# A gated mix of a long convolution and a dilated local attention: projection in halves, convolution with three buffers, and another order of loads and requests

## The chip, the cores and the metric

The kernel runs on one core of one Trainium2 chip. The core has five engines, each with its own in-order list of instructions: TensorE (PE in the profile; its weight loads are PEld), VectorE (DVE), ScalarE (ACT), GpSimd (POOL) and SyncE (SP). SyncE, ScalarE and GpSimd also issue DMA transfers, which 16 DMA engines carry out. The metric is the device time of one execution in microseconds, median of several; less is better.

## What is computed

The inputs have 2048 positions and 640 channels, in bf16. With x = q, the output is g * a + (1 - g) * b, in short:

```python
g = sigmoid((x * gate_w).sum(-1, keepdims=True))
# a: a short convolution of 4 taps on k, times v, then a long convolution over all positions
k_shift = sum(k_pad[:, t:t+S, :] * shift_k[:, 3 - t] for t in range(4))
kv = k_shift * v
y  = irfft(rfft(kv, 2*S) * rfft(ssm_k, 2*S))[:S] + kv * ssm_D
a  = q * y
# b: attention of 32 heads of 20 channels, each position looks at 8 positions, 2 apart
q_, k_, v_ = split(x @ wqkv)
attn = softmax(q_ . k_[pos - 2*w] * 20**-0.5, w = 0..7)
b = (attn . v_[pos - 2*w]) @ wo
```

## The kernel before

The attention half. Even and odd positions are taken apart, so that a head looks at 8 neighbours in a row. `xpose` turns x (tile `xn`) into `xT` by TensorE. `qkproj` makes q and k (five tiles `ft` of 128 columns, first with `Wqk`'s first 128 columns and then the rest), evicted into `stg`; `vproj` makes v in two halves of 320 columns (tile `psv`, evicted into `VW`). `fragger` copies each head's 20 rows from `stg` into a set of four heads (`kb`, `qb`), by DMA issued from GpSimd (line 583). The sets already hold, in other rows, factors that make the mask: GpSimd's `masks` (lines 362 to 365) spreads them from the small tile `mm` over three sets, at the start of the kernel, ahead of the first head's copy on GpSimd's list. Then `score_gen` multiplies (tile `sc`, line 607), ScalarE takes the exponential into `ETall` (line 614), `pv_gen` multiplies by v (tile `O`, line 637), and VectorE divides (lines 647 and 650). There are 80 such groups of scores. `op_tr` and `outproj` (tiles `tr`, `op`, `bl`) are the projection by `wo`.

The convolution half. `conv` (line 453) makes the four taps on VectorE: it first rearranges the tap weights, which GpSimd's queue loads from `shift_k` (line 406), by the copy of line 455, and then works on pieces of CR rows of k (tile `KX`), from the last row to the first. In `taps` a multiplication (line 440) writes one of two buffers, and an addition (line 447) adds it to the other. k arrives in three parts (`KROWS`), the first of them, rows 42 to 63, at the start. `conv_v` multiplies by v. The long convolution is a transform by matrices in two steps on TensorE (`h_stream`, `u_stream`, tiles `H`, `SX`, `UC`, `s`), a product on VectorE (line 717) and an inverse (line 796, tile `i`; last step line 877, `final`).

What sets the order. Each part is a Python generator that asks for its next request: TensorE, or ScalarE or VectorE for an eviction, and so on. The string `ORDER` grants these requests one by one (a letter for each generator, "-" ahead of it for the second engine named, VectorE), and the instructions are written in that order; nothing is decided while the kernel runs. Costs in the requests and the numbers in `LAND` and `STARTS` are not used by the chip: they are what the string was worked out from. Every engine works through its list in order, and waits where an operand is not there. TensorE's results go through four pairs of PSUM banks, which the evictions free.

`heads` (line 367) issues what comes first: the first loads from the queues of ScalarE and SyncE, the small loads of GpSimd, and the masks.

Of the kernel before, what the change touches and what calls it, by code (L numbers as in the profile page):

```python
# [12 lines left out]
ACT = mybir.ActivationFunctionType  # L13
ALU = mybir.AluOpType
# [3 lines left out]
S = 2048  # L18
D = 640
# [3 lines left out]
NDT = 5  # L23
# [94 lines left out]
fcddccfcccccccxfdccfedddcccciccccdxxxeicxxxcccffcfccffdeffffxddxdddxx-xddffdffdiiddddxxeddeddfiddd-idi-idddeecccddilddddd-iicccycy  # L118
yf-icccc-yxycfcccccccccc-xfccccccyyyiydcccdeicc-yyyeycyiidddffdxddddxid-ideeddffdidddddcccc-iiffciyyeddecdfiddcd-idccdccccccfccffi
yyyyfici-ii-idddceddddeccccjdddffdidcdjdiedgddcccdigedddgdcccii-idycdccde-ydeddy-yccyycyddd-ydy-yyylyjdcecyccccccdjgdccdddjyceddd  # L120
-yydd-ydddz-zzzz-zzzeeddyd-yyddd-yz-zddzzz-zzzz-zzzedddzjdedd-zccddddzd-zdeedzddd-zz-zddzddde-zddddedz-zzzzjzeeqzzz-z000-00z00oopo
oooo-z00-0110-00001o-1o0000-0111-11101-010-0001o10-0110-0000oo11022211oooor-rpr2rr20-r0r1-r1112r-r2200o2011s0s22222222u001111s2s11
22o2111ss1ss111111o2ou4444444oo4ss33443333s333334444444444u33333333333u555suuuvuuuuuuuvvv5v5-5v5-55vvvvv555v55555-555ttst-tsssttvv
tt-ttttsss-sttt-ttsttts-tttssttttttsss-ssttst-ttts-st
"""


# [70 lines left out]
def kernel(  # L198
# [14 lines left out]
    nc = tc.nc  # L213
# [44 lines left out]
    pab = pab.rearrange("p (a n c) -> p a n c", a=2, c=QC)  # L258
# [28 lines left out]
    def ev(name):  # L287
        if name not in E:
            E[name] = Ev()
        return E[name]  # L290
# [5 lines left out]
    def at(name, t):  # L296
        ev(name).src, ev(name).lag = -1, t

    st = {}
# [67 lines left out]
    def heads():  # L367
# [6 lines left out]
        nc.scalar.dma_start(mm[:], ca["mm"].ap())  # L374
        for w in range(2):
            nc.scalar.dma_start(Wqk[:, :, w, 0:128], W3[:, :, w, 0:128])
            at(f"W0{w}", LAND["W0"])
        nc.scalar.dma_start(Wv[:, :, 0:320], W3[:, :, 2, 0:320])
        at("Wv0", LAND["Wv0"])
        at("ET", 4000.0)  # L380
        for a in range(8):
            nc.sync.dma_start(xn[:, a], raw(x2, 256 * a * D, [[2 * D, 128], [D, 2], [1, D]]))
            at(f"x{a}", LAND["x"][a])
        for w in range(2):
# [4 lines left out]
        n0, n1 = KROWS[0]  # L389
        for q in range(4):  # L390
            nc.sync.dma_start(kin[32 * q:32 * q + 32, 3 + n0:3 + n1, :], raw(k2, n0 * D + QC * q, [[64 * D, 32], [D, n1 - n0], [1, QC]]))
        for q in range(4):
            at(f"k0{q}", LAND["k"][0])
# [43 lines left out]
    def taps(eng, n, m, ta, tb, dst):  # L437
        def tap(d, j):
            w = wl[:, j, :].unsqueeze(1)
            eng.tensor_tensor(d, kin[:, n + 3 - j:n + 3 - j + m, :], w.to_broadcast([128, m, QC]), ALU.mult)  # L440

        tap(ta, 3)
        for j in (2, 1, 0):
            yield
            tap(tb, j)
            yield
            eng.tensor_tensor(ta if j else dst, ta, tb, ALU.add)  # L447

    def vmul(eng, n, m, c, ks):
        v_ = vin[:, c, n:n + m, :]  # L450
# [2 lines left out]
    def conv():  # L453
        yield Req("D", 570.0, [ev("k00")])
        nc.vector.tensor_copy(wl, wraw.rearrange("p c j -> p j c"))
        hi = 64
        while hi:
            m = min(CR, hi)
            n = hi - m
            c0 = 150.0 + 0.54 * m * QC  # L460
            need = [k for k, (n0, n1) in enumerate(KROWS) if n0 < hi and n1 > n - 3]
            g = yield Req("D", c0, [ev(f"k{k}{q}") for k in need for q in range(4)] + ([ev(f"kh{q}{a}") for q in range(4) for a in (1, 17)] if n < 3 else []))
            for _ in taps(nc.vector, n, m, pab[:, 0, 0:m], pab[:, 1, 0:m], kin[:, n + 3:n + 3 + m, :]):
                g = yield Req("D", c0)
            hi = n
        mark("convD", g)

# [352 lines left out]
    def outproj():  # L820
        yield Req("N", 0.0, [ev("oTall"), ev("wo"), ev("gate")])
        bl = p0.tile([128, 16, D], BF, name="bl", tag="VW")
        st["bl"] = bl
        wo, oT = st["wo"], st["oT"]
        for t in range(16):
            g = yield Req("P", 0.0, [ev(f"oT{ft}") for ft in range(NDT)], take=1, pe=(10, 149.0, 280.0, 133.0))
            op = psum(g, "op", (128, 1024))
            for ft in range(NDT):
                for n0, n1 in ((0, 512), (512, 640)):
                    nc.tensor.matmul(op[:, n0:n1], lhsT=oT[:, ft].rearrange("p h m a -> p a (h m)")[:, t, :], rhs=wo[:, ft, n0:n1],  # L830
                                     start=(ft == 0), stop=(ft == NDT - 1), skip_group_check=True)
            r = yield Req("AD", dict(A=680.0, D=740.0), [g.done], give=g.banks)
            if r.eng == "A":
                nc.scalar.activation(bl[:, t, :], op[:, 0:D], ACT.Copy, scale=omg[:, t:t + 1])
            else:
                nc.vector.tensor_scalar(bl[:, t, :], op[:, 0:D], omg[:, t:t + 1], None, ALU.mult)
            mark(f"bl{t}", r)
        mark("outproj", g)

# [95 lines left out]
```

## Time and profile before

| | us |
|---|---|
| median of 3 runs (225.1 to 226.12) | 226.06 |
| the profiled execution's own time | 226.44 |
| its span, from the first to the last instruction | 224.5 |
| TensorE busy | 204.4 (91%) |
| VectorE busy | 183.1 (82%) |
| ScalarE busy | 171.0 (76%) |
| GpSimd busy | 69.0 (31%) |

The granted TensorE clock is 0.999 over the span. The stages: to 31 us the transposes and first projections; 31 to 143 us scores, exponentials and values, with the convolution, the other projections and the transform of the filter in between; 143 to 197 us the transform of the signal, the products, the output projection and the inverse; then the final stage with the output's DMAs. In the profile a row of the timeline has the start, the length, the engine, the line, the operation, the tiles written and read, the number of instructions, and in brackets how long the engine had stood and what ended it. In the chain of waits a row is a stretch of the chain that ended last. TensorE's busy time includes the time that a matmul takes to run out, so 91% is not 91% of its peak.

### The profile page before, as it was taken

To read this page: it belongs to the slowest core of one execution; us is meant where nothing else is said; L and a number is where in the kernel's file an instruction comes from. 1 tells how busy PE (TensorE), PEld (TensorE's weight loads), DVE (VectorE), ACT (ScalarE), POOL (GpSimd) and SP (SyncE) were. 2 spreads that over 40 slices of the span, in tenths; PEclk is the share of its full clock that TensorE was granted. 3 is DMA by queue.
4 is the path that set the end of the run, shared out by engine and by line. 5 is a ranking of instruction groups with operands and counts; after the bars stand their busy time and mean duration, and the time that the engine had idled before them with its cause. 6 is when DMAs were issued, how large, how long until landed. Compare 5 with 4: busy or idle time off the path is not lost.

```text
span 224.5 us, 8412 instructions
## 1 busy us (share of the span) xinstructions
PE 204.4 (91%) x3644; PEld 160.9 (72%) x3653; DVE 183.1 (82%) x236; ACT 171.0 (76%) x208; POOL 69.0 (31%) x154
## 2 busy tenths in 40 slices
PE   6799979999999979999998889879999999979890
PEld 2687966689776756666676667778987989967660
DVE  4533564889988966999899988999999997769982
ACT  2475437776978589879899989899999989755640
POOL 1999961534007614072360000000120094000000
PEclk9999999999999999999999999999999999999999
DMA  6999459999999989849944085584969404004544
GB/s 211 359 339 199 83 133 194 175 163 163 194 184 217 190 148 145 118 110 164 177 109 141 14 217 127 117 216 116 243 145 194 109 12 104 20 3 103 139 125 109
DMA packets 69020, 33.83 MB, mean 151 GB/s; under 512 B 51096, under 2 KB 66600, under 8 KB 68984
## 3 DMA queue, kind: packets, MB, share of 16 engines
q1 hardware_dynamic: 63192, 26.79, 57.0%
q0 software_dynamic: 3536, 5.69, 11.6%
q10 hardware_dynamic: 2256, 0.83, 1.5%
q8 instruction: 28, 0.46, 1.0%
q14 instruction: 8, 0.07, 0.1%
HBM read 20.01 MB, written 2.62 MB: 101 GB/s over the span
## 4 chain that ended last, share of the span: by engine, by line
PE 40%; DVE 21%; POOL 11%; issue 11%; DMA 8%; ACT 6%; ACTq 0%; DVEq 0%; POOLq 0%
PE pj L535 9%; PE i L796 8%; PE s L685 5%; ACT ETall L614 4%; PE O L637 4%; DVE UC L227 4%; PE op L830 4%; DMA qb<-stg 4%; PE psv L486 3%; DVE H L227 3%; DMA kb<-stg 3%; POOL qb L365 2%; PE sc L607 2%; DVE SX L227 2%; POOL qb L583 2%
## 5 line engine op out<-in xcount | busy, mean ns | idle before, releaser
L614 ACT ACTIVATE ETall<-sc 121x912 bf16<-121x912 f32 (+1 forms) x80 | 63.7, 860 | 13.5 <-PE sc L607 13.2
L535 PE MATMUL pj<-xT,Wqk 128*128 128x342 bf16 (+1 forms) x300 | 47.9, 310 | 0.4 <-ACT xT L225 0.3
L535 PEld LDWEIGHTS <-Wqk 128*128 128x128 bf16 x300 | 27.8, 97 | 15.1 <-issue 0.4
L583 POOL DMA_DIRECT2D qb<-stg x36 | 18.1, 503 | 43.2 <-ACT ETall L614 21.8
L440 DVE TENSOR_TENSOR KX<-KX 128x1760 bf16<-128x1760 bf16 (+1 forms) x24 | 24.6, 1041 | 8.1 <-DMA KX<-in_A_k_dram 7.8
L225 ACT CAST UC<-s 128x960 bf16<-128x960 f32 (+2 forms) x32 | 28.9, 994 | 0.1
L486 PE MATMUL psv<-WvT,xT 128*121 128x320 bf16 x180 | 26.6, 301 | 0.0
L830 PE MATMUL op<-wo,oT 128*128 128x128 bf16 (+1 forms) x151 | 24.0, 301 | 0.6
L486 PEld LDWEIGHTS <-xT 128*121 128x121 bf16 x180 | 23.4, 134 | 1.1
L607 PE MATMUL sc<-qb,kb 31*128 31x114 bf16 x576 | 20.9, 212 | 2.7 <-DMA kb<-stg 1.5
L685 PEld LDWEIGHTS <-G 64*128 64x128 bf16 x512 | 18.3, 93 | 4.7 <-issue 2.6
L830 PEld LDWEIGHTS <-oT 128*128 128x128 bf16 x160 | 16.4, 147 | 6.0
L607 PEld LDWEIGHTS <-kb 31*128 31x128 bf16 x576 | 12.4, 93 | 11.6 <-issue 6.9
L583 POOL DMA_DIRECT2D kb<-stg x36 | 17.9, 502 | 8.3 <-ACT ETall L614 2.6
L447 DVE TENSOR_TENSOR KX<-KX 128x1760 bf16<-128x1760 bf16 (+1 forms) x18 | 18.8, 1046 | 0.5
L225 ACT CAST stg<-pj 128x684 bf16<-128x684 f32 (+1 forms) x19 | 14.2, 754 | 6.1 <-PE pj L535 4.1
L637 PE MATMUL O<-VW,ETall 121*128 121x63 bf16 (+2 forms) x576 | 18.2, 184 | 0.4 <-DVE stg L227 0.3
L637 PEld LDWEIGHTS <-ETall 121*128 121x128 bf16 x576 | 17.1, 96 | 1.8 <-issue 0.3
L225 ACT CAST UC<-i 128x1024 bf16<-128x1024 f32 x17 | 16.3, 1049 | 2.6 <-PE i L796 2.6
L796 PE MATMUL i<-F,Hw 128*128 128x128 bf16 x160 | 18.2, 219 | 0.0
L796 PEld LDWEIGHTS <-Hw 128*128 128x128 bf16 x160 | 17.9, 114 | 0.0
L775 POOL COPY Hw<-Hw 128x1 bf16<-128x1 bf16 x6 | 1.6, 259 | 48.4 <-DMA Hw<-H 27.9
(80 smaller groups left out, 360.0 us busy)
## 6 DMA issues: line engine op xcount, KB each, us to landing
xn<-in_A_q_dram SPq DMA_DIRECT2D x8, 320.0 KB, 5.7
h_lin<-in_A_ssm_k_dram SPq DMA_DIRECT2D x16, 160.0 KB, 5.0
vin<-in_A_v_dram SPq DMA_DIRECT2D x8, 320.0 KB, 7.5
Hw<-H SPq DMA_DIRECT2D x8, 320.0 KB, 4.1
Hw<-SX SPq DMA_DIRECT2D x8, 320.0 KB, 4.6
q<-in_A_q_dram SPq DMA_DIRECT2D x8, 320.0 KB, 5.0
kb<-stg POOLq DMA_DIRECT2D x28, 85.1 KB, 4.9
qb<-stg POOLq DMA_DIRECT2D x28, 80.2 KB, 4.8
```

Of the source, the lines that this page charges most:

```text
L225: nc.scalar.copy(dst, src)
L227: nc.vector.tensor_copy(dst, src)
L440: eng.tensor_tensor(d, kin[:, n + 3 - j:n + 3 - j + m, :], w.to_broadcast([128, m, QC]), ALU.mult)
L486: nc.tensor.matmul(ps[0:BK, par, 0:320], lhsT=xT[:, dt, s0:s0 + BK], rhs=Wv[:, dt, 320 * hp:320 * hp + 320], start=(dt == 0), stop=(dt == ...
L535: nc.tensor.matmul(ps[:, i, 0:n], lhsT=Wqk[:, dt, w, 128 * ft:128 * ft + 128], rhs=xT[:, dt, s0:s0 + n], start=(dt == 0), stop=(dt == NDT ...
L583: nc.gpsimd.dma_start(dst[r0:r0 + rows, 0:wd], stg[fa - f0:fb - f0, 0:wd])
L607: nc.tensor.matmul(sc[:, hh, BQ * bb:BQ * bb + BQ], lhsT=kb[r:r + DH + NF, BK * b:BK * b + 128], rhs=qb[r:r + DH + NF, BQ * b:BQ * b + BQ] ...
L614: nc.scalar.activation(ETall[0:BK, e, :, 0:BQ * nb], sc[0:BK, :, 0:BQ * nb], ACT.Exp, scale=SCALE)
L637: nc.tensor.matmul(O[:, (b - b0) // 6, c0:c0 + 21 * nh], lhsT=ETall[0:BK, e, hh, BQ * bb:BQ * bb + 128], rhs=VW[0:BK, b, 4 * t + h4:4 * t ...
L685: nc.tensor.matmul(ps[:, c, 160 * jj:160 * jj + 160], lhsT=G[rows, j0 + jj, rr, :], rhs=Am[rows, rr].rearrange("p o (q j) l -> p j (o q) l ...
L796: nc.tensor.matmul(d, lhsT=st[(key, P)][:, c, o + il // 4, :, il % 4], rhs=M[:, k, :], start=(k == 0), stop=(k == 1), skip_group_check=True)
L830: nc.tensor.matmul(op[:, n0:n1], lhsT=oT[:, ft].rearrange("p h m a -> p a (h m)")[:, t, :], rhs=wo[:, ft, n0:n1], start=(ft == 0), stop=(f ...
```

## The change

Four things change.

- The first loads. ScalarE's queue issues `ident`, `Wv`'s first half, `Wqk`'s first 128 columns and then `mm`; SyncE's queue issues x, then the first rows of k, then the rest of `Wqk` and `Wv`.
- The convolution works in pieces of 8 rows (CR) with three buffers in place of 11 rows with two: 56 operations in place of 42. Three multiplications come first, and then additions and the last multiplication alternate.
- The output projection computes two halves of 320 columns, each in its own PSUM bank, in place of 512 and 128 columns.
- The string `ORDER` is another one, and with it the list of every engine.

```diff
-CR = 11
+CR = 8
-LAND = dict(W0=8700.0, Wv0=12000.0, W1=17900.0, Wv1=19500.0, x=[4300.0, 5300.0, 6800.0, 8000.0, 10200.0, 11300.0, 12300.0, 13100.0], k=[23500.0])
-STARTS = dict(P=5100.0, A=5600.0, D=7500.0, G=23500.0, S=20000.0)
+LAND = dict(W0=8900.0, Wv0=6600.0, W1=22500.0, Wv1=24500.0, x=[4300.0, 5300.0, 7500.0, 8800.0, 10200.0, 11300.0, 12300.0, 13100.0], k=[18800.0])
+STARTS = dict(P=5100.0, A=5600.0, D=7500.0, G=23500.0, S=24000.0)
...
-a-aaaaaa-ai-iaaiaaiwa-aaaiiiiiiciiccccc-wwwcwwfcccccccccccwwfffwwwwcw-ww-wccdcddwdddddwiicidcffffccccccdddiiiiiiiieiccdccccccccccf
+aaa-awa-awwa-aawaiia-aaaaai-iififfffffffiiffiiiifcwwwcccccccwfwwwww-wfw-wdfdcccdwccdddcdc-wccccidddcccc-icccccccccccdidddde-iciiii
...
-    sizes = [67 * QC, 2 * CR * QC, 4 * QC]
+    sizes = [67 * QC, 3 * CR * QC, 4 * QC]
...
-        nc.scalar.dma_start(mm[:], ca["mm"].ap())
+        nc.scalar.dma_start(Wv[:, :, 0:320], W3[:, :, 2, 0:320])
+        at("Wv0", LAND["Wv0"])
         for w in range(2):
             nc.scalar.dma_start(Wqk[:, :, w, 0:128], W3[:, :, w, 0:128])
...
-        nc.scalar.dma_start(Wv[:, :, 0:320], W3[:, :, 2, 0:320])
-        at("Wv0", LAND["Wv0"])
...
             nc.sync.dma_start(xn[:, a], raw(x2, 256 * a * D, [[2 * D, 128], [D, 2], [1, D]]))
             at(f"x{a}", LAND["x"][a])
+        nc.scalar.dma_start(mm[:], ca["mm"].ap())
+        n0, n1 = KROWS[0]
+        for q in range(4):
+            nc.sync.dma_start(kin[32 * q:32 * q + 32, 3 + n0:3 + n1, :], raw(k2, n0 * D + QC * q, [[64 * D, 32], [D, n1 - n0], [1, QC]]))
...
-        tap(ta, 3)
-        for j in (2, 1, 0):
-            yield
-            tap(tb, j)
-            yield
-            eng.tensor_tensor(ta if j else dst, ta, tb, ALU.add)
+        ta, tb, tc_ = t3
+        tap(ta, 3)
+        yield 0
+        tap(tb, 2)
+        yield 0
+        tap(tc_, 1)
+        yield 0
+        eng.tensor_tensor(ta, ta, tb, ALU.add)
+        yield 110.0
+        tap(tb, 0)
+        yield 0
+        eng.tensor_tensor(ta, ta, tc_, ALU.add)
+        yield 110.0
+        eng.tensor_tensor(dst, ta, tb, ALU.add)
...
-            c0 = 150.0 + 0.54 * m * QC
+            c0 = 72.0 + 0.523 * m * QC
...
-            op = psum(g, "op", (128, 1024))
+            op = psum(g, "op")
             for ft in range(NDT):
-                for n0, n1 in ((0, 512), (512, 640)):
-                    nc.tensor.matmul(op[:, n0:n1], lhsT=oT[:, ft].rearrange("p h m a -> p a (h m)")[:, t, :], rhs=wo[:, ft, n0:n1],
+                for n in range(2):
+                    nc.tensor.matmul(op[:, n, 0:320], lhsT=oT[:, ft].rearrange("p h m a -> p a (h m)")[:, t, :], rhs=wo[:, ft, 320 * n:320 * n + 320],
```

How the lists move is seen at three places. First ScalarE's, at the start of the program: `ident` is the identity for the transposes, `mm` the mask factors, `WvT` the weights of v, `tx` the transposed x. Before:

```order
L373 DMA ident<-ca_ident 128x128
L374 DMA mm<-ca_mm 128x235
L376 DMA Wqk<-in_B_wqkv_dram 128x5x128 x2
L378 DMA WvT<-in_B_wqkv_dram 128x5x320
L225 ACT_TABLE_LOAD
L225 COPY xT<-tx 128x2x5x128 x4
```

and with the change:

```order
L373 DMA ident<-ca_ident 128x128
L374 DMA WvT<-in_B_wqkv_dram 128x5x320
L377 DMA Wqk<-in_B_wqkv_dram 128x5x128 x2
L383 DMA mm<-ca_mm 128x235
L225 ACT_TABLE_LOAD
L225 COPY xT<-tx 128x2x5x128
```

The load of `mm` has moved behind three larger loads of the same queue. GpSimd's own list, which begins with copies from `mm`, stands as before.

Second SyncE's list, its first rows. Before:

```order
L382 DMA xn<-in_A_q_dram 128x1280 x8
L385 DMA Wqk<-in_B_wqkv_dram 128x5x512 x2
L387 DMA WvT<-in_B_wqkv_dram 128x5x320
L391 DMA KX<-in_A_k_dram 32x22x160 x4
L303 DMA KX<-in_A_k_dram 32x22x160 x4
```

and with the change:

```order
L381 DMA xn<-in_A_q_dram 128x1280 x8
L386 DMA KX<-in_A_k_dram 32x22x160 x4
L390 DMA Wqk<-in_B_wqkv_dram 128x5x512 x2
L392 DMA WvT<-in_B_wqkv_dram 128x5x320
L303 DMA KX<-in_A_k_dram 32x22x160 x4
```

The first rows of k have moved ahead of the weights.

Third VectorE's list from the rearrangement of the tap weights on (`KX` holds k and the buffers, `psv` the projected v), before:

```order
L455 COPY KX<-KX 128x640
L440 TENSOR_TENSOR KX<-KX 128x1760 x2
L447 TENSOR_TENSOR KX<-KX 128x1760
L227 CAST VW<-psv 121x2x16x20 x2
L440 TENSOR_TENSOR KX<-KX 128x1760
L447 TENSOR_TENSOR KX<-KX 128x1760
L440 TENSOR_TENSOR KX<-KX 128x1760
L447 TENSOR_TENSOR KX<-KX 128x1760
```

and with the change:

```order
L463 COPY KX<-KX 128x640
L440 TENSOR_TENSOR KX<-KX 128x1280 x3
L449 TENSOR_TENSOR KX<-KX 128x1280
L440 TENSOR_TENSOR KX<-KX 128x1280
L453 TENSOR_TENSOR KX<-KX 128x1280
L455 TENSOR_TENSOR KX<-KX 128x1280
L440 TENSOR_TENSOR KX<-KX 128x1280 x3
L449 TENSOR_TENSOR KX<-KX 128x1280
L440 TENSOR_TENSOR KX<-KX 128x1280
L227 CAST VW<-psv 121x2x16x20
L453 TENSOR_TENSOR KX<-KX 128x1280
```

Twelve operations of the convolution stand ahead of the first eviction of `psv`, where three stood; the multiplications of line 440 come three in a row.

More of the change, by code (lines that the diff above doesn't have):

```diff
@@ L383, in heads @@
             at(f"x{a}", LAND["x"][a])
+        nc.scalar.dma_start(mm[:], ca["mm"].ap())
+        n0, n1 = KROWS[0]
+        for q in range(4):
+            nc.sync.dma_start(kin[32 * q:32 * q + 32, 3 + n0:3 + n1, :], raw(k2, n0 * D + QC * q, [[64 * D, 32], [D, n1 - n0], [1, QC]]))
+        for q in range(4):
+            at(f"k0{q}", LAND["k"][0])
         for w in range(2):
@@ L388, in heads @@
         at("Wv1", LAND["Wv1"])
[L389 to L393, printed above, removed]
         nc.gpsimd.memset(xT[:, :, 0:X0], 0.0)
@@ L459, in conv @@
             n = hi - m
-            c0 = 150.0 + 0.54 * m * QC
+            c0 = 72.0 + 0.523 * m * QC
             need = [k for k, (n0, n1) in enumerate(KROWS) if n0 < hi and n1 > n - 3]
             g = yield Req("D", c0, [ev(f"k{k}{q}") for k in need for q in range(4)] + ([ev(f"kh{q}{a}") for q in range(4) for a in (1, 17)] if n < 3 else []))
-            for _ in taps(nc.vector, n, m, pab[:, 0, 0:m], pab[:, 1, 0:m], kin[:, n + 3:n + 3 + m, :]):
-                g = yield Req("D", c0)
+            for more in taps(nc.vector, n, m, [pab[:, i, 0:m] for i in range(3)], kin[:, n + 3:n + 3 + m, :]):
+                g = yield Req("D", c0 + more)
             hi = n
@@ L825, in outproj @@
         for t in range(16):
[L826 to L827 removed]
+            g = yield Req("P", 0.0, [ev(f"oT{ft}") for ft in range(NDT)], take=1, pe=(10, 137.0, 272.0, 133.0))
+            op = psum(g, "op")
             for ft in range(NDT):
[L829 to L830 removed]
+                for n in range(2):
+                    nc.tensor.matmul(op[:, n, 0:320], lhsT=oT[:, ft].rearrange("p h m a -> p a (h m)")[:, t, :], rhs=wo[:, ft, 320 * n:320 * n + 320],
                                      start=(ft == 0), stop=(ft == NDT - 1), skip_group_check=True)
             r = yield Req("AD", dict(A=680.0, D=740.0), [g.done], give=g.banks)
+            dst = bl[:, t].rearrange("p (a n) -> p a n", a=2)
             if r.eng == "A":
[L834 removed]
+                nc.scalar.activation(dst, op[:, :, 0:320], ACT.Copy, scale=omg[:, t:t + 1])
             else:
[L836 removed]
+                nc.vector.tensor_scalar(dst, op[:, :, 0:320], omg[:, t:t + 1], None, ALU.mult)
             mark(f"bl{t}", r)
```

18 lines of the change are left out of this document (9 added, 9 removed).

## The prediction

> **What bounds the kernel now.** I read the chain that ended last first, because it says which work the end hangs on, and its first 34 us name one transfer and one engine. The columns are start, length, and what was done.
>
> ```profile
> 1.15 3.93 DMA mm<-ca_mm
> 5.13 2.00 POOL kb L364
> 7.14 1.84 POOL qb L365
> ...
> 13.48 1.94 POOL kb L364
> 15.41 1.84 POOL qb L365
> ...
> 22.47 1.96 POOL Dz L412 x4
> 27.99 5.10 DMA kb<-stg
> 33.52 1.50 PE psv L486 x10
> ```
>
> The chain starts with the load of `mm`, goes through GpSimd's mask copies, small loads and copies of heads (`kb<-stg`), and reaches TensorE only at 33.5 us. Next the timeline of that stretch, rows of several engines:
>
> ```profile
> 1.15 0.45 ACTq L374 DMA_DIRECT2D mm<-ca_mm  x1
> 1.63 1.10 ACTq L376 DMA_DIRECT2D Wqk<-in_B_wqkv_dram  x2
> 3.92 0.37 ACTq L378 DMA_DIRECT2D WvT<-in_B_wqkv_dram  x1
> 5.13 2.00 POOL L364 COPY kb<-mm 128x2178 bf16<-128x2178 bf16 x1 [3.98 <-DMA mm<-ca_mm]
> ...
> 19.51 1.92 DVE L455 COPY KX<-KX 128x640 bf16<-128x640 bf16 x1 [2.84 <-DMA KX<-in_A_shift_k_dram]
> ...
> 24.41 0.52 POOL L583 DMA_DIRECT2D qb<-stg  x1
> ...
> 25.18 2.06 DVE L440 TENSOR_TENSOR KX<-KX 128x1760 bf16<-128x1760 bf16 x2 [3.75 <-DMA KX<-in_A_k_dram]
> ...
> 27.27 1.07 DVE L447 TENSOR_TENSOR KX<-KX 128x1760 bf16<-128x1760 bf16 x1
> ...
> 30.96 0.45 PE L607 MATMUL sc<-qb,kb 31*128 31x114 bf16 x8
> ...
> 33.14 0.38 PE L607 MATMUL sc<-qb,kb 31*128 31x114 bf16 x7 [0.70 <-DMA kb<-stg]
> 33.45 1.57 PE L486 MATMUL psv<-WvT,xT 128*121 128x320 bf16 x10
> ```
>
> GpSimd stood 3.98 us until `mm` was there, and from 5.13 to its first copy of a head at 24.41 it has 19.28 us of work. TensorE comes to the first scores at 30.96, just when the heads land. So GpSimd and TensorE arrive together here, with no slack on either. Last, the busy time by stretch (columns: stretch, length, busy us of PE, weight loads, DVE, ACT, POOL, clock, DMA):
>
> ```profile
> 33.40:100.00 66.60, 65.36 (x947) 47.46 (x942) 55.96 (x67) 51.70 (x67) 23.98 (x69) 1.00 0.98 167
> 100.00:143.40 43.40, 38.80 (x954) 29.63 (x942) 40.61 (x51) 41.00 (x53) 7.91 (x25) 1.00 0.63 140
> 143.40:197.00 53.60, 51.39 (x922) 46.31 (x921) 50.97 (x81) 50.83 (x58) 10.17 (x12) 1.00 0.53 123
> 197.00:224.50 27.50, 19.99 (x606) 14.80 (x612) 20.36 (x22) 12.12 (x15) 0.00 (x0) 0.99 0.39 98
> ```
>
> From the first scores to 100 us TensorE is busy in 65.36 of 66.60: it is the bound, and 1.24 us is all it loses. From 100 to 143 VectorE and ScalarE are both 94% busy, then all three near 95%, and the last 27.5 us go by VectorE (20.36 against 12.12 on ScalarE). What is lost before 33 us can therefore be won back only where VectorE or ScalarE bounds.
>
> **The change, part by part.**
>
> *The order of the first loads on ScalarE's queue.* `mm` now stands behind `ident`, `Wv` and both `Wqk` pieces instead of ahead of them. What that queue (q10) moved before, in 0 to 4, 4 to 8.4, and 8.4 to 11.3 us (packets, MB, share of the 16 DMA engines):
>
> ```profile
> q10 hardware_dynamic: 270, 0.09, 8.5%
> ...
> q10 hardware_dynamic: 1646, 0.54, 51.3%
> ...
> q10 hardware_dynamic: 340, 0.21, 22.7%
> ```
>
> That is 0.84 MB by 11.3 us, and the queue has nothing afterwards. The first 0.09 MB are `ident` and `mm`: the transfers are served in their order. With the same 0.84 MB and `mm` last, `mm` lands when the queue ends, near 11.3 us at the latest. At the earliest: the new table of the change expects `Wqk` at 8.9 us, and `mm`, 58.8 KB at the queue's 0.54 MB in 4.4 us, takes 0.5 us more, with some landing time 9.7. I take 10.5, nearer the middle: 5.4 us later than 5.13, bounds 4.6 and 6.2. GpSimd has the same list behind it, so its first copy of a head goes out at 29.8 in place of 24.41, and the first scores can start at 36.4 in place of 30.96, those of heads 2 and 3 at 38.5 in place of 33.14. TensorE has the same work ahead of its first score in both programs (80 transposes, 60 `pj`, 80 `psv` matmuls), so it arrives at about 31 to 32 and stands for some 4 to 5 us, then another 2 ahead of the second group. Queued behind: all of its list, in a fixed order. ScalarE waits for it with the exponentials. Cost where TensorE bounds: +5.4.
>
> *The order on SyncE's queue.* The rows 42 to 63 of k now go ahead of `Wqk` and the second half of `Wv`, expected at 18.8 us. In the trace VectorE waited 3.75 us for k, after 2.84 us for `shift_k`. But `shift_k` is loaded by GpSimd behind the first mask pair, so it too comes 5.4 us later: the rearrangement of weights (1.92 us) starts near 24.9, and the convolution near 26.8 instead of 25.18. The early k buys nothing at its start. The later `Wqk` (22.5 by the table) is first used behind the first scores: nothing, cover 14 us.
>
> *The convolution in pieces of 8 with three buffers.* Rows that give its prices:
>
> ```profile
> 32.90 1.07 DVE L447 TENSOR_TENSOR KX<-KX 128x1760 bf16<-128x1760 bf16 x1
> 34.01 1.07 DVE L440 TENSOR_TENSOR KX<-KX 128x1760 bf16<-128x1760 bf16 x1
> ...
> 208.14 0.82 DVE L889 TENSOR_TENSOR q<-yb,q 128x1280 bf16<-128x1280 bf16 x1
> 209.00 0.82 DVE L891 TENSOR_TENSOR q<-q,bl 128x1280 bf16<-128x1280 bf16 x1
> 209.74 1.15 DVE L227 CAST yb<-i 128x960 bf16<-128x960 f32 x1
> ```
>
> An operation that needs its predecessor starts 1.11 us after it at 1760 elements (32.90 to 34.01), 0.86 at 1280 (208.14 to 209.00). One that doesn't starts 0.74 after a 1280 (209.00 to 209.74); the pair at 25.18 with its successor at 27.27 says 0.98 for 1760. Before: five pieces of 0.98 + 6 x 1.11 and one of nine rows (0.82 + 6 x 0.94, scaled to 1440 elements), 44.7 us. After: eight of 5 x 0.74 + 2 x 0.86, 43.4. So -1.3 at best. If taking the chain apart saved nothing, 56 x 0.86 = 48.2 would stand against 35 x 1.11 + 7 x 0.94 = 45.4: +2.8 at worst. The rows at 25.18 and 209.00 are of this very kind, so the value lies near the lower end; with the first operation of a piece waiting for the piece ahead (8 x 0.12) it is -0.3, and as it lies on VectorE beside a bound TensorE, I take 0.
> The Trainium skill ("VectorE: DVE Perf Modes", section "The DRAIN you can't avoid") speaks against this part: each operation waits until the pipe is empty, and chaining or not makes no difference. By it the worse end would hold, 2.8 us on VectorE; the pair at 25.18, two operations of 1.07 in 2.06, disagrees.
>
> *VectorE's order.* Ahead of the second group of scores 14 of 56 convolution operations stand in its list, two whole pieces, where 5 of 42 stood. Two pieces are 2 x 5.42 = 10.8 us, five operations of 1.07 are 5.4: a lead of 5.4 us by 38.5 us, as VectorE works while TensorE stands. What is it worth? At the least nothing, since TensorE bounds until 100 us; at most 5.4, if VectorE alone set the time. I take 1.2, which is all the idle time TensorE has in 33.4 to 100: ahead of the 41st of 80 score groups both lists have nearly all of the convolution (40 of 42, and 55 of 56), so the lead is used up where TensorE bounds.
>
> *Output projection in two halves of 320.* One unit of ten matmuls each way, and the same with 320 columns in `psv`:
>
> ```profile
> 46.32 1.50 PE psv L486 x10
> ...
> 168.74 1.54 PE op L830 x10
> ```
>
> 1.54 against 1.50 us: 0.04 a unit, 16 units, -0.6 on TensorE in stretches it nearly fills (bounds 0 and -0.6). The eviction reads the same 640 values, as `psv`'s does from two banks: nothing.
> The Trainium skill ("TensorE: Matmul & The Clock Gate", section "Back-to-back issue gap") gives 81 ns sustained at 128 columns and 131 at 512. A line between them puts 320 at 106, so 212 ns a pair either way and no gain: 0.6 more. The trace's 154 ns a matmul is far from that 106.
>
> *The requests in a new order.* In the tail VectorE's list loses one eviction `yb` (1.15 us, the row at 209.74) and one `bl` to ScalarE, which is 44% busy there:
>
> ```profile
> 206.51 0.80 DVE bl L836
> ```
>
> Together -2.0 at most, and 0 at least; I take half, as the rest waits on TensorE. SyncE's list has `wo` and the tables `T` further back, behind copies of `Hw`; they are first used by `op` (the unit at 168.74 is an early one) and by the final stage after 197, so nothing, and if `wo` came later than `op`'s turn, TensorE would stand there. From 143 to 197 both lists hold the same evictions and products: 0, and a reordering alone could move it a microsecond either way.
>
> Sum: 5.4 - 1.2 + 0 - 0.6 - 1.0 = +2.6 us. The profiled execution's own time is 226.44 (span 224.5, 1.9 around it), which gives 229.0; the median of the runs is 226.06, and against it I say 228.7.
>
> **The rivals.**
>
> *VectorE's lead is the bound's own (faster).* If in 33 to 143 us VectorE sets the pace after all, its lead of 5.4 comes off in full. For it: 94% busy after 100 us. Against: ScalarE is equally busy there, and TensorE at 98% ahead of it. 5.4 - 5.4 - 0.6 - 1.0 = -1.6, 224.5 us. It decides from 4.9 us recovered (5.4 - 4.9 - 1.6 is -1.1, half a per cent). Chance 0.13.
>
> *Half of the lead counts.* ScalarE and VectorE share evictions, so 5.4 freed on one is 2.7 on both: 5.4 - 2.7 - 1.6 = +1.1, and with the early bound for `mm` +0.3: between, 226.8. Chance 0.15.
>
> *`mm` is not late.* If small packets of one queue pass the large ones ahead, GpSimd starts as before, the convolution starts near 21.4, and only gains remain: -0.6 - 1.0 = -1.6, with the 1.2 of the lead -2.8; 223.9 us between them. Against: the 0.09 MB came first and alone. Chance 0.08.
>
> *No recovery, and dearer operations.* With the later bound for `mm`, nothing regained in the tail or the lead: 6.2 - 0.6 = +5.6, 231.7 us. A convolution at its worse end comes out alike: 2.6 + 2.8, 231.5. Chance 0.10 for the two together.
>
> **How the numbers follow.** My forecast holds the remaining 0.54, with its own range of 227.3 to 231. 0.5% is about what can be told from no change here, so 224.9 to 227.2. Faster: 0.13 + 0.08, less a little that ends short of it, 0.19. Same: 0.15 and small parts of its neighbours, 0.18. Slower: 0.63. The range reaches from 224.3, inside the two faster rivals, to 231.7, the dearest one.
>
> **What would show it.** After: GpSimd's wait for `mm` near 9 us instead of 3.98; the first copy of a head near 29.8; TensorE idle 4 us or more on `kb<-stg` ahead of its first score at about 36; `shift_k` holding VectorE until near 25; then the last `O` matmuls some 4 us later than before, at 147. An `op` unit of 1.50, 1280-wide convolution operations 0.74 apart. I am wrong if `mm` lands before 7 us, or if the scores' end is not later in spite of a late start; then the order behind it, which I costed at 1.2 us, was worth more than I read from the stretches.

## The result and the profile after

The changed kernel takes 233.24 us (median of 4 executions, 233.13 to 236.11), the kernel before beside it 226.09 (225.1 to 226.46): a ratio of 1.035, with a 95% interval of 1.027 to 1.044. Ratios, here and below, leave out disturbed executions, and so are not always the quotient of the medians. The direction is the one forecast, the size is not: +7.2 us instead of +2.6, above the range. The profiled execution is the 236.11; its span is 234.3.

First the busy times and the granted clock in 40 slices, from the page of the kernel before:

```profile
PE 204.4 (91%) x3644; PEld 160.9 (72%) x3653; DVE 183.1 (82%) x236; ACT 171.0 (76%) x208; POOL 69.0 (31%) x154
...
PEclk9999999999999999999999999999999999999999
```

and from that of the changed kernel:

```profile
PE 210.9 (90%) x3653; PEld 169.9 (73%) x3653; DVE 185.7 (79%) x251; ACT 171.3 (73%) x207; POOL 76.3 (33%) x154
...
PEclk9999995899999999999999955899999999999996
```

TensorE is busy for 6.5 us more with the same work (3653 weight loads on both pages; the count of 3644 matmuls before lacks nine records). The clock line says why: before it was 9 in every slice, now it falls in slices 7 and 8 (to half, from 35.7 to 42.5 us), again near 140, and at the end. Then the timeline of the stretch that the forecast was about, several engines, the first columns start and length:

```profile
10.80 2.00 POOL L364 COPY kb<-mm 128x2178 bf16<-128x2178 bf16 x1 [9.65 <-DMA mm<-ca_mm]
...
23.95 1.29 DVE L463 COPY KX<-KX 128x640 bf16<-128x640 bf16 x1 [6.42 <-DMA KX<-in_A_shift_k_dram]
24.83 2.17 POOL L365 COPY qb<-mm 128x2052 bf16<-128x2052 bf16 x1
25.28 3.87 DVE L440 TENSOR_TENSOR KX<-KX 128x1280 bf16<-128x1280 bf16 x3
...
30.35 0.51 POOL L591 DMA_DIRECT2D qb<-stg  x1
...
33.60 0.20 PE L615 MATMUL sc<-qb,kb 31*128 31x114 bf16 x1 [2.98 <-DMA kb<-stg]
33.80 0.50 POOL L591 DMA_DIRECT2D kb<-stg  x1
...
34.79 0.38 PE L615 MATMUL sc<-qb,kb 31*128 31x114 bf16 x7 [0.98 <-DMA kb<-stg]
36.17 0.27 PE L615 MATMUL sc<-qb,kb 31*128 31x114 bf16 x1 [1.00 <-ACT ETall L622]
37.36 0.56 PE L615 MATMUL sc<-qb,kb 31*128 31x114 bf16 x7 [0.92 <-DMA kb<-stg]
37.85 2.92 PE L494 MATMUL psv<-WvT,xT 128*121 128x320 bf16 x10
```

`mm` lands at 10.80 instead of 5.13, the first copy of a head goes out at 30.35 instead of 24.41, and TensorE stands four times, 5.88 us together (1.51 in the kernel before, ahead of its third and fourth head). The last row is the one that the forecast lacks: ten `psv` matmuls took 1.57 us before at this place and take 2.92 here. The busy times around it (stretch, length, PE, weight loads, DVE, ACT, POOL, clock, DMA), changed kernel:

```profile
28.85:32.26 3.41, 1.77 (x14) 1.45 (x11) 3.34 (x5) 0.00 (x0) 3.41 (x8) 1.00 0.29 38
32.27:35.68 3.41, 0.58 (x8) 0.30 (x8) 3.34 (x6) 0.48 (x1) 3.41 (x8) 1.00 0.56 144
35.69:42.51 6.82, 5.42 (x39) 3.56 (x40) 4.33 (x6) 2.58 (x4) 2.83 (x20) 0.50 1.01 174
42.52:45.93 3.41, 3.41 (x57) 2.08 (x55) 1.42 (x2) 2.58 (x4) 0.00 (x0) 1.00 1.34 196
```

In every trace of this study the halved stretches last 3.41 us or a multiple of it, but for the last one, which the end of the program cuts off; so the windows are cut in such steps. TensorE is busy for 0.58 us of the step from 32.27 on, a sixth of it. In the next two steps the clock is 0.50, in the one after it is whole again. From 33.40 to 43.00 TensorE starts 51 matmuls; before it started 97:

```profile
33.40:43.00 9.60, 9.60 (x97) 6.50 (x93) 5.40 (x6) 7.67 (x10) 1.97 (x15) 1.00 1.11 190
```

and after:

```profile
33.40:43.00 9.60, 6.49 (x51) 4.16 (x52) 6.58 (x9) 3.56 (x4) 5.12 (x24) 0.64 0.92 170
```

The last `O` matmul ends at 152.28 us, before at 143.56.

### The profile page after: what moved, and what is told of

It is laid out like the page before. It is cut to its first block, busy times and chain, and to the rows that moved or that the text cites. A ratio compares the mean times of both kernels' runs of the same rounds, so it can differ in the third digit from the quotient of the medians.

```text
span 234.3 us, 8437 instructions
## 1 busy us (share of the span) xinstructions
PE 210.9 (90%) x3653; PEld 169.9 (73%) x3653; DVE 185.7 (79%) x251; ACT 171.3 (73%) x207; POOL 76.3 (33%) x154
## 5 line engine op out<-in xcount | busy, mean ns | idle before, releaser
L622 ACT ACTIVATE ETall<-sc 121x912 bf16<-121x912 f32 (+1 forms) x80 | 65.0, 860 | 21.7 <-PE sc L615 21.0
L591 POOL DMA_DIRECT2D qb<-stg x36 | 18.0, 502 | 44.9 <-ACT stg L225 29.8
L615 PE MATMUL sc<-qb,kb 31*128 31x114 bf16 x576 | 22.6, 226 | 7.6 <-DMA kb<-stg 5.5
L440 DVE TENSOR_TENSOR KX<-KX 128x1280 bf16<-128x1280 bf16 x32 | 26.8, 873 | 0.4
L838 PE MATMUL op<-wo,oT 128*128 128x320 bf16 x160 | 23.7, 302 | 0.1
L838 PEld LDWEIGHTS <-oT 128*128 128x128 bf16 x160 | 21.2, 145 | 0.9
L591 POOL DMA_DIRECT2D kb<-stg x36 | 17.9, 503 | 10.5 <-ACT ETall L622 5.7
L856 POOL COPY link<-q 32x1 bf16<-32x1 bf16 x4 | 15.8, 3942 | 13.6 <-DMA q<-in_A_q_dram 13.6
L645 PEld LDWEIGHTS <-ETall 121*128 121x128 bf16 x576 | 18.5, 100 | 1.8 <-issue 0.5
L227 DVE CAST stg<-pj 128x726 bf16<-128x726 f32 (+1 forms) x14 | 12.5, 890 | 9.3 <-PE pj L543 6.8
L645 PE MATMUL O<-VW,ETall 121*128 121x63 bf16 (+2 forms) x576 | 19.7, 190 | 0.1
L225 ACT CAST stg<-pj 128x684 bf16<-128x684 f32 (+1 forms) x16 | 12.0, 753 | 8.0 <-PE pj L543 8.0
```

The source lines that it names most:

```text
L225: nc.scalar.copy(dst, src)
L591: nc.gpsimd.dma_start(dst[r0:r0 + rows, 0:wd], stg[fa - f0:fb - f0, 0:wd])
L615: nc.tensor.matmul(sc[:, hh, BQ * bb:BQ * bb + BQ], lhsT=kb[r:r + DH + NF, BK * b:BK * b + 128], rhs=qb[r:r + DH + NF, BQ * b:BQ * b + BQ] ...
L622: nc.scalar.activation(ETall[0:BK, e, :, 0:BQ * nb], sc[0:BK, :, 0:BQ * nb], ACT.Exp, scale=SCALE)
L645: nc.tensor.matmul(O[:, (b - b0) // 6, c0:c0 + 21 * nh], lhsT=ETall[0:BK, e, hh, BQ * bb:BQ * bb + 128], rhs=VW[0:BK, b, 4 * t + h4:4 * t ...
L838: nc.tensor.matmul(op[:, n, 0:320], lhsT=oT[:, ft].rearrange("p h m a -> p a (h m)")[:, t, :], rhs=wo[:, ft, 320 * n:320 * n + 320], start ...
```

## The experiments

How often and where the clock is halved differs between executions of one kernel (before: 224.85 to 230.94 us in 69 of them). Hence beside the medians stand, where it matters, those of the executions with a mean clock of 0.99 or more; for them the kernel before has 225.95 (43 of the 69). They are picked by the clock, so they answer only the question of what a kernel takes when the clock is kept.

### Is the late load of `mm` the whole loss?

**e1_mm_second**: the changed kernel, `mm` issued as the second transfer of ScalarE's queue again.

```diff
+        nc.scalar.dma_start(mm[:], ca["mm"].ap())
         nc.scalar.dma_start(Wv[:, :, 0:320], W3[:, :, 2, 0:320])
...
-        nc.scalar.dma_start(mm[:], ca["mm"].ap())
```

> The changed kernel, with the load of mm issued second on ScalarE's queue as before the change; all else as changed. Theory A (the late mm costs twice: GpSimd's list starts 5.7 us later, so TensorE stands ahead of the first scores, and the standing halves its clock for 6.8 us): mm lands near 5.1 us, GpSimd's first copy of a head goes out near 24.5, no half clock ahead of 130 us, and the time comes back to 224.5 to 227 us. Theory B (the new list of instructions and the order of SyncE's queue are worse in themselves, the start matters little): 230 us or more.

Measured: 228.01 us over 10 executions, ratio to before 1.000 (0.996 to 1.005). Most of the loss is gone, though the median of all ten is still 1.3 above the 226.73 of the kernel before beside it. The profile shows that this place has a price too:

```profile
4.64 2.00 POOL L364 COPY kb<-mm 128x2178 bf16<-128x2178 bf16 x1 [3.48 <-DMA mm<-ca_mm]
9.99 2.82 PE L494 MATMUL psv<-WvT,xT 128*121 128x320 bf16 x10 [3.92 <-DMA WvT<-in_B_wqkv_dram]
```

Now `Wv` comes later, TensorE stands 3.92 us for it, and the clock is halved from 8.0 to 14.8. So not all went as expected: the first copy of a head goes out only at 26.95, because GpSimd now waits for the evictions of q and k (3.03 us on ScalarE's `stg`), and the first exponential is 4.4 us later than in the kernel before. By the 30th exponential the kernel is level with before all the same (0.2 us). That is not because the delay costs nothing: beside e5 below, the same list with `mm` elsewhere, it is 3.6 us late at the 6th exponential and still 3.6 at the 30th. The new list is about that much ahead of the old one there.

**e5_mm_on_sync**: `mm` on SyncE's queue, right behind the first piece of x.

```diff
             nc.sync.dma_start(xn[:, a], raw(x2, 256 * a * D, [[2 * D, 128], [D, 2], [1, D]]))
+            if a == 0:
+                nc.sync.dma_start(mm[:], ca["mm"].ap())
...
-        nc.scalar.dma_start(mm[:], ca["mm"].ap())
```

> The changed kernel with mm issued on SyncE's queue, right after the first piece of x, so that ScalarE's queue still brings Wv first (in the first kernel with an early mm, Wv came at 10 us and TensorE stood 3.9 us for it). Theory A: mm lands by 5.5 us, GpSimd's first copy of a head goes out near 25, TensorE reaches the first scores near 31 to 32 and neither stands there nor at 6 to 10 us, no half clock ahead of 130 us. If the rest of the change is worth something once the start is mended: 223 to 225.5 us. If it is worth nothing: 226 to 227, as the kernel before.

Measured: 225.45 us (10 executions), before beside it 226.46, ratio 0.994 (0.989 to 0.998). `mm` is there at 4.00 us. One moved load thus makes the whole difference between +3.5% and none or a small gain.

**e11_before_mm_sync**: the same edit in the kernel before, to see whether the load alone gives e5's gain; and **e12_mm_sync_again**, e5's kernel beside it.

> The kernel before with mm issued on SyncE's queue right after the first piece of x, as in e5; nothing else. It tells how much of e5's gain of 1.4 us over the kernel before comes from the load itself, 1.1 us earlier there (4.00 against 5.13), and how much from the rest of the change. Theory A (the rest of the change, its order and the halves of op, is worth the gain): GpSimd starts near 4.0, its first copy of a head goes out near 23.3, but TensorE comes to the first scores no earlier than about 30.5, so no more than 0.5 us is gained: 225.5 to 226.5, and e5 stays below it by 0.5 to 1.5. Theory B (the earlier masks are the gain): GpSimd and TensorE stood tied, the whole chain moves up by about 1 us, 224.5 to 225.4, and e5 is the same as this kernel.

> The same kernel as e5, on the same chip and beside the same runs of the kernel before as e11, so that the two can be compared: under theory A 224.7 to 225.6, 0.5 to 1.5 below e11; under theory B within 0.5 of e11. In both no stand of TensorE over 1.5 us ahead of the first scores and no halved clock before 100 us.

Measured: 227.7 (ratio 1.005, 1.001 to 1.009) and 226.9 (0.998, 0.993 to 1.003), 12 executions each, before 226.17. Theory B falls: in the old list the earlier `mm` brings nothing, it costs half a per cent. x comes later behind it, and the expectation that the clock is not halved early is missed. TensorE's timeline in e11:

```profile
8.24 0.73 PE L421 MATMUL tx<-ident,xn 128*128 128x128 bf16 x10 [0.77 <-DMA xn<-in_A_q_dram]
9.64 1.25 PE L421 MATMUL tx<-ident,xn 128*128 128x128 bf16 x10 [0.67 <-DMA xn<-in_A_q_dram]
10.68 2.68 PE L536 MATMUL pj<-xT,Wqk 128*128 128x342 bf16 x10
```

TensorE stands between its transposes, and the first `pj` group takes 2.68 us where it took 1.6: the clock is halved from 9.4 to 12.8. Theory A's gain is not confirmed either: e12 lies 0.8 below e11, but its interval against the kernel before holds 1. Over e5 and e12 the changed kernel with `mm` on SyncE's queue has 226.18 (22 executions) against 226.38 (42): with `mm` on time, the rest of the change is worth nothing that these runs can tell.

**e2_before_mm_last**: the converse, the kernel before with only `mm` moved behind `Wv` on ScalarE's queue.

```diff
-        nc.scalar.dma_start(mm[:], ca["mm"].ap())
...
         nc.scalar.dma_start(Wv[:, :, 0:320], W3[:, :, 2, 0:320])
+        nc.scalar.dma_start(mm[:], ca["mm"].ap())
```

> The kernel before, with one line moved: mm is issued last on ScalarE's queue. Theory A: GpSimd's first copy of a head near 30, TensorE stands some 3 us at the first scores, half clock for two steps of 3.4 us soon after, time 231 to 234 us. If lateness alone counts and the clock doesn't: 230 to 231. Theory B: 226 to 228 us.

Measured: 234.88 us over 4 executions, ratio 1.033 (1.023 to 1.043), as the whole change. The clock is halved from 35.1 to 42.0. In the old list this one line alone makes a loss of the same size.

### What does the wait cost, and what the clock?

**e3_filled**: the changed kernel, `mm` as late, but with dummy matmuls (xT by xT, 512 columns) ahead of the first score of each of the first four heads, 14, 5, 5 and 5 of them, into the bank that this score overwrites. They end about when the heads land; no work is left out.

```diff
+FILL = (14, 5, 5, 5)
...
+                            if s < 2 and not bb:
+                                for _ in range(FILL[2 * k + hh]):
+                                    nc.tensor.matmul(sc[:, hh, :], lhsT=xT[:, 0, 16:144], rhs=xT[:, 0, 16:528],
+                                                     start=True, stop=True, skip_group_check=True)
```

> The changed kernel; ahead of the first score of each of the four heads of the first set TensorE multiplies x by itself 14, 5, 5 and 5 times (512 columns, 213 ns each), into banks that the scores overwrite, so that it isn't idle while it waits for the heads. The heads come as late as in the changed kernel. Theory A: no half clock near 36 to 42 us, and 2 to 3.4 us come back: 230 to 231.3 us. If the half clock costs nothing (it only covers waits): 233.2 us, as changed, or some tenths more.

Measured: 229.29 us over 10 executions, ratio 1.010 (1.005 to 1.015); 228.6 where the clock was kept. TensorE's timeline:

```profile
30.53 3.19 PE L618 MATMUL sc<-xT 128*128 128x512 bf16 x13
33.65 0.22 PE L620 MATMUL sc<-qb,kb 31*128 31x114 bf16 x1
33.80 1.25 PE L618 MATMUL sc<-xT 128*128 128x512 bf16 x5
...
38.12 1.57 PE L495 MATMUL psv<-WvT,xT 128*121 128x320 bf16 x10
```

The score of the first head comes at 33.65 as in the changed kernel (33.60), so the wait is untouched; the `psv` group behind takes 1.57 us again. Useless work of TensorE made the kernel 4 to 4.6 us faster.

**e10_filled_once**: the same with FILL = (14, 0, 0, 0): the one long stand is filled, the three short ones stay.

```diff
-FILL = (14, 5, 5, 5)
+FILL = (14, 0, 0, 0)
```

> The changed kernel with the filling ahead of the first head alone (14 multiplications; none ahead of the other three). TensorE is then busy until 33.6 us, and from there to 37.4 does 1.4 us of work in 3.8. If it takes one long stand of about 3 us to halve the clock: none, 228.5 to 229.5 us, as with all four filled. If what counts is how much TensorE works in a step of 3.4 us (the steps with 0.15 to 0.53 of busy time were followed by half clock, those with 0.57 and more in this part of the kernel were not), it depends on where the step falls, and some or all executions have half clock: 230.5 to 233 us.

Measured: 232.4 us, ratio 1.026 (1.020 to 1.033). Its timeline of TensorE and its windows:

```profile
34.69 0.38 PE L620 MATMUL sc<-qb,kb 31*128 31x114 bf16 x7 [0.83 <-DMA kb<-stg]
35.99 0.22 PE L620 MATMUL sc<-qb,kb 31*128 31x114 bf16 x1 [0.93 <-DMA kb<-stg]
37.45 0.56 PE L620 MATMUL sc<-qb,kb 31*128 31x114 bf16 x7 [1.25 <-DMA kb<-stg]
```

```profile
30.14:33.55 3.41, 3.36 (x18) 1.61 (x16) 3.34 (x5) 0.00 (x0) 3.41 (x7) 1.00 0.45 91
33.56:36.97 3.41, 0.89 (x10) 0.40 (x9) 3.38 (x6) 0.93 (x1) 3.41 (x8) 1.00 0.61 155
36.98:43.80 6.82, 6.35 (x42) 4.10 (x43) 2.80 (x4) 2.68 (x3) 1.31 (x17) 0.50 1.15 182
```

No stand there is longer than 1.25 us, and still the clock halves, 1.3 us later than in the changed kernel, behind the step in which TensorE is busy for 0.89 of 3.41 us. So one long stand is not needed: it is enough that TensorE does little within a step. The Trainium skill ("TensorE: Matmul & The Clock Gate", section "HAM oscillation — how this bites in real kernels") puts the rule as no idle gaps over about 3.4 us; here gaps of 2.98 us at most, and in e10 of 1.25, were enough, and the measurement decides.

**e9_before_last_filled**: e2 with the dummy matmuls of e3, in these numbers:

```diff
+FILL = (9, 5, 5, 5)
```

> The kernel before with mm issued last on ScalarE's queue, and TensorE filled ahead of the first score of each of the first four heads with 9, 5, 5 and 5 multiplications of x by itself (213 ns each), into banks that the scores overwrite. This parts the wait from the clock in the old list. Theory A: the first scores are 4 to 5 us late as without the filling, no half clock near 35 to 42 us, so the time is 3 to 4.5 us above the kernel before, 229.5 to 231; with the half clock it was 232 to 235. If the half clock is not what costs there: as without the filling.

Measured: 232.77 us over 4 executions, ratio 1.031 (1.026 to 1.036), the clock whole until the end; 229.5 to 231 was expected, a miss. Filling brings only 2 us here, against 4 to 4.6 in the new list. Where the profiled executions are along the way, by the start of ScalarE's n-th exponential and the end of the last `O` matmul, in us, each less the same point of the kernel before:

| start or end (us in before) | after | e3 (filled) | e10 (once) | e2 | e9 (filled) | e6 (`mm` early) |
|---|---|---|---|---|---|---|
| 1st exponential (31.45) | 3.75 | 3.95 | 3.65 | 4.05 | 4.39 | -0.19 |
| 6th (39.55) | 5.08 | 3.22 | 5.79 | 6.40 | 5.11 | -2.25 |
| 16th (60.88) | 7.50 | 4.49 | 7.07 | 6.25 | 5.73 | -0.97 |
| 30th (84.09) | 5.45 | 2.47 | 5.06 | 5.66 | 5.09 | -2.99 |
| 60th (120.27) | 4.92 | 2.26 | 4.52 | 5.66 | 5.10 | -3.23 |
| last `O` (143.56) | 8.72 | 3.67 | 5.09 | 5.67 | 5.10 | -2.68 |
| span (224.52) | 9.81 | 3.56 | 5.32 | 5.67 | 5.33 | -2.10 |

In the old list the wait alone, at a whole clock, costs 5.1 us in the profile and keeps them to the end. The profiled executions of e2 and e9 are the fastest of their four, though: e9's median is 6.8 above the 225.95 of the kernel before at a kept clock. The halving adds 0.6 in these profiles, 2.1 in the medians. In the new list the wait costs 5.5 at the 60th exponential (e3 less e6; later e3 has a halved step, at 132.8, and e6 has none), and the halving another 3.0 from the 16th exponential to the 30th, 2.7 at the 60th (after less e3). Why the halving costs more in the new list I can't show: in both lists some 40 matmuls are started in the two halved steps.

The 8.72 at the last `O` holds a second halved stretch of the profiled execution, 134.6 to 148.3. The median doesn't hang on it: two of the three other executions, 233.13 and 233.26, have a mean clock of 0.973 and 0.975, which is some 12 us at half, about the first stretch and the end. The third, 233.22, has 0.951, some 10 us more at half, and is no slower. So not every halved stretch costs time; where its stretches lie no trace shows.

### The rest of the change

**e4_small_loads_first** (e1 with GpSimd's small loads, `shift_k` among them, ahead of the first mask pair) and **e6_mm_sync_small_first** (the same on e5). Both in GpSimd's part of `heads`:

```diff
-        masks(0)
...
+        masks(0)
```

The call goes from ahead of the small loads to behind them.

> As the first kernel of this set (mm issued second), and on GpSimd's list the small memsets and the four loads of shift_k stand ahead of the first masks, in the time in which GpSimd waits for mm. GpSimd's first copy of a head then goes out near 21 to 22 us, the tap weights land by 14, and the convolution starts by 21 (k is expected at 18.8) in place of 25. Theory A, in which start and scores hang on GpSimd: TensorE no longer waits for heads (0.8 us and 0.7 us less), VectorE's lead is 4 us larger: 223 to 225.5 us. If TensorE's own list sets the time from 5 to 100 us, nothing but the two waits: within 1 us of the first kernel of this set.

> As the kernel with mm on SyncE's queue, and GpSimd's small memsets and loads of shift_k stand ahead of its first masks. GpSimd is ready for the heads by 21 to 22 us, and the convolution starts near 19.5 to 20.5 in place of 22 to 23. If VectorE's lead is worth anything: 0.5 to 1.5 us below the kernel with mm on SyncE's queue alone; if TensorE bounds until 100 us: within 0.5 us of it.

Measured: e4 231.62 us over 4 executions, ratio 1.023 (1.014 to 1.031), a miss: `Wv` came later still (10.98, a stand of 4.89), the clock was halved from 8.0 to 14.9 and once more at 131. e6: 226.44 us over 10 executions, ratio 0.996 (0.990 to 1.002), the same as e5 within what can be told. It doesn't test VectorE's lead: the tap weights are ready earlier, but now the convolution waits for k, and starts at 20.29 as in e5 (20.31). Its profiled execution, 222.4 us of span, is the one of the new list without a halved step before the end, and it shows the convolution undisturbed (VectorE's timeline):

```profile
17.74 0.48 DVE L464 COPY KX<-KX 128x640 bf16<-128x640 bf16 x1
20.29 2.30 DVE L441 TENSOR_TENSOR KX<-KX 128x1280 bf16<-128x1280 bf16 x3 [2.07 <-DMA KX<-in_A_k_dram]
22.50 0.82 DVE L450 TENSOR_TENSOR KX<-KX 128x1280 bf16<-128x1280 bf16 x1
23.36 0.82 DVE L441 TENSOR_TENSOR KX<-KX 128x1280 bf16<-128x1280 bf16 x1
24.10 0.82 DVE L454 TENSOR_TENSOR KX<-KX 128x1280 bf16<-128x1280 bf16 x1
24.95 0.82 DVE L456 TENSOR_TENSOR KX<-KX 128x1280 bf16<-128x1280 bf16 x1
25.81 2.29 DVE L441 TENSOR_TENSOR KX<-KX 128x1280 bf16<-128x1280 bf16 x3
```

A piece of seven operations takes 5.52 us: they start 0.74 apart where an operation does not need the one ahead, 0.85 where it does.

**e7_two_buffers**: e5 with the old chain of two buffers in pieces of 8. One execution.

```diff
-        tap(tb, 2)
-        yield 0
-        tap(tc_, 1)
-        yield 0
-        eng.tensor_tensor(ta, ta, tb, ALU.add)
...
+        for j in (2, 1, 0):
+            yield 0
+            tap(tb, j)
+            yield 0
+            eng.tensor_tensor(ta if j else dst, ta, tb, ALU.add)
```

> As the kernel with mm on SyncE's queue, but the pieces of 8 rows use two buffers in the old order, so each operation needs the one ahead of it. By the rows of the kernel before, a piece takes 0.74 + 6 x 0.86 = 5.9 us of VectorE in place of 5.42 where nothing stands between, 8 pieces 3.8 us more at the most; read from the starts of the convolution's operations. In the time: 0 to 1.5 us more.

Measured: 227.45 us. The whole convolution, from each operation's start to the next one on VectorE's list with waits left out, takes 46.0 us; with three buffers 43.77 (e5 and e6), in the kernel before 43.72. So the third buffer saves 2.2 us and the smaller pieces cost as much.

**e8_k_last**: e5 with the first rows of k issued behind the weights again. One execution.

```diff
-        n0, n1 = KROWS[0]
-        for q in range(4):
-            nc.sync.dma_start(kin[32 * q:32 * q + 32, 3 + n0:3 + n1, :], raw(k2, n0 * D + QC * q, [[64 * D, 32], [D, n1 - n0], [1, QC]]))
...
         nc.sync.dma_start(Wv[:, :, 320:640], W3[:, :, 2, 320:640])
...
+        n0, n1 = KROWS[0]
+        for q in range(4):
+            nc.sync.dma_start(kin[32 * q:32 * q + 32, 3 + n0:3 + n1, :], raw(k2, n0 * D + QC * q, [[64 * D, 32], [D, n1 - n0], [1, QC]]))
```

> As the kernel with mm on SyncE's queue, but the first rows of k are issued behind Wqk and Wv on SyncE's queue, as before the change. k lands near 24 and the convolution starts near 25 in place of 22 to 23. If VectorE's lead is worth its size: 2 us more; if TensorE bounds until 100 us: 0 to 0.5 us more.

Measured: 233.87 us, where 2 us more than e5 was the most expected: a miss. The convolution starts at 26.19, and TensorE's timeline says what that does:

```profile
32.77 0.38 PE L616 MATMUL sc<-qb,kb 31*128 31x114 bf16 x7 [0.95 <-DMA kb<-stg]
36.39 2.82 PE L495 MATMUL psv<-WvT,xT 128*121 128x320 bf16 x10 [3.24 <-DVE VW L227]
```

With twelve operations of the convolution ahead of the first eviction of `psv` in VectorE's list, a late k holds up the evictions, TensorE stands 3.24 us for a bank, and the clock is halved from 33.2 to 40.0. In the new list k must be early, as far as one execution shows it.

## Why the prediction was right and wrong

- **`mm` late, by the order of the queue: right.** 10.80 us against 10.5 forecast; GpSimd's wait 9.65 against "near 9"; the first copy of a head 30.35 against 29.8. e2 and e5 show that this is the cause. The rival "`mm` is not late" falls.
- **First scores at 36.4: wrong, they start at 33.60.** The forecast passed the whole lateness of GpSimd on to TensorE, with "no slack on either". For the first head there was slack: in the kernel before its `kb` landed at 27.51 and TensorE came only at 30.96. For the others there was none: the second head landed at 30.99, the fourth at 33.09. With the change these landed at 34.74 and 37.32, only 3.75 and 4.23 us later, though their copies went out 5.8 later. The copies themselves were quicker: the fourth head's `kb` took 5.10 us before (27.99 in the chain of the prediction) and 3.5 after (33.80, first used at 37.36). The forecast took that time as fixed; what shortened it, I can't show. So the `psv` matmuls behind these scores start at 37.85 instead of 33.45, 4.4 us late and not 5.4.
- **"Cost where TensorE bounds: +5.4": a wait of about this size came, but what it does to the clock was left out.** This is the step by which the forecast missed. The halved clock comes on top of the wait, 3 us in the profiles and 233.24 - 228.6 = 4.6 in the times, and the forecast had no term for it, though it had TensorE standing 4 to 5 us and more. Where the clock is kept, the changed kernel with its late load has 228.6 us (e3, 5 of 10 executions), which is +2.6 on the kernel before (225.95), as much as the whole sum of the forecast. That the two meet is partly luck. With 224.5 for the same kernel with `mm` early (e5, e6, e12; 14 of 32 executions), the wait is 228.6 - 224.5 = +4.1 where +5.4 was forecast, and the rest 224.5 - 225.95 = -1.4 where -2.8 was: two errors of 1.3 and 1.4 that cancel. The profiles say 5.7 for the wait and -2.1 for the rest (spans of e3, e6 and before).
- **Recovery of 1.2 by VectorE's lead: the direction holds, the cause is not shown.** In e5 and e6 the convolution starts 4.9 us earlier than before and ends 4.7 to 5.1 earlier; the last `O` ends 0.9 to 2.7 earlier and the span is 0.1 to 2.1 shorter. A lead of 5 us is not worth 5, so the rival that VectorE sets the pace falls. But e6, the one without a halved step on the way, has 2.7 at the last `O`, as much as the rival "Half of the lead counts". The two lists differ in more than VectorE's order, and no run changes that order alone.
- **"The early k buys nothing": wrong for this list.** At its own place it was right (weights rearranged from 23.95, forecast 24.9; convolution at 25.28, forecast 26.8), but e8 shows that without it the evictions behind it would hold up TensorE. I asked what the earlier transfer gives and not what the new list needs.
- **Convolution 0: right**, 43.77 against 43.72 us; independent operations 0.74 apart, as forecast. Taking the chain apart is worth 46.0 - 43.8 = 2.2 us of VectorE (e7), so the prediction's worse end does not hold. The section of the Trainium skill that the prediction sets against it ("VectorE: DVE Perf Modes", "The DRAIN you can't avoid") itself adds that a next operation that is not held starts earlier; the prediction left that out.
- **Halves of `op` -0.6: right.** A unit on its own in TensorE's timeline, before and after:

```profile
168.68 1.61 PE L830 MATMUL op<-wo,oT 128*128 128x512 bf16 x10
```

```profile
178.78 1.58 PE L838 MATMUL op<-wo,oT 128*128 128x320 bf16 x10
```

  0.03 us a unit, 0.5 over 16 units; too little to be told in the times.
- **Tail -1.0: too much.** From the start of the final step to the end of the span: 26.8 us before, 26.3 to 26.6 in e3, e5 and e6, so -0.2 to -0.5.

What stays open: the halved stretches between 115 and 148 us that most profiles of the new list show (after, e3, e4, e5, e7, e8, e12). Of the old list the profiles of the kernel before, e2 and e9 have none there and e11 has one at 128.9; 13 of the 69 executions of the kernel before have a mean clock under 0.98, more than a halved step at the end explains, so it is not free of such stretches either. The steps ahead of these stretches have TensorE busy for 69 to 82%, but others with 53 to 63% kept the clock, the one at 28.85 shown above among them, so no threshold in busy time explains them. They are a likely reason why the new list's 1.4 us at a kept clock do not show in its medians: of the 32 executions with `mm` early, 14 are at 0.99 or more, with a median of 224.5, and the other 18 have 226.9. Whether they can be avoided was not tried.

## What to carry to other kernels

When an edit makes TensorE stand, look at how much it still does in 3.4 us around that place: steps busy for up to 42% were always followed by a halved clock here, steps between 42 and 53% some of the time, and in the changed kernel this cost 3 to 5 us beyond the stand itself. If the stand can't be removed, some throw-away matmuls that end about when the operand lands are worth more than the idle time (here 228.6 to 229.3 against 233.2 us; 2 us in the old list). A small load on which a long in-order list hangs belongs ahead of large ones, but what is pushed back by it must be looked at too: `Wv` in e1, x in e11.

## What the runs showed of the hardware that was not expected

- The clock changes in steps of 3.41 us, and a poor step is paid for in the following ones: 0.58, 0.89 and 0.52 busy of 3.41 us (after, e10, e2) were each followed by 6.8 us at half. In the fourteen profiles every step with up to 1.44 us was followed by a halved one. Between 1.45 and 1.79 it went both ways: 1.45 (before, at 217.02), 1.53 (e10, at 221.32) and 1.77 (after, at 28.85) were not followed by it, 1.68 (e11, at 6.01) and 1.79 (e8, at 29.78) were.
- VectorE is slowed by GpSimd's mask copies. The rearrangement of the tap weights takes 0.48 us alone (e6, at 17.74) and 1.92 in the kernel before, where it runs beside such a copy:

```profile
19.17 1.91 POOL L365 COPY qb<-mm 128x2052 bf16<-128x2052 bf16 x1
19.51 1.92 DVE L455 COPY KX<-KX 128x640 bf16<-128x640 bf16 x1 [2.84 <-DMA KX<-in_A_shift_k_dram]
```

  Here it ends 0.35 us after GpSimd's copy (21.43 and 21.08), and so it does in the changed kernel (25.24 and 24.89) and in e5 (20.28 and 19.93): it looks like waiting for that copy rather than like running slower. In the changed kernel the first three multiplications take 3.87 us beside the copy at 24.83, and 2.30 in e6 without one. The Trainium skill ("SBUF — State Buffer", section "Who interferes with whom") says that VectorE's copies can contend with GpSimd for a shared port pair, that its instructions with two inputs in SBUF contend with a GpSimd instruction that reads SBUF, and that for the whole of one instruction the other can be blocked; these rows agree. The forecast took the 1.92 us as the operation's own length.
